# Cluster attention on one core: four of six first tiles split on GpSimd, and masks, v's splits, moves and loads placed anew

## The chip, the cores and the metric

The program runs on one core of a Trainium2 chip. The time is device microseconds of one execution; before the change the median of three runs is 765.99 us (765.26 to 767.38). The core has five engines with a queue each: TensorE (PE, with its weight loads shown apart as PEld), VectorE (DVE), ScalarE (ACT), GpSimd (POOL) and SyncE (SP), which here only issues DMAs.

## The reference

Three stages follow each other. Attention has 2 batches, 8 heads, 768 rows and a head dimension of 64; a row of q sees only rows of k that fall to the same of 16 centroids. Then come two feed-forward stages on 1536 tokens.

```python
mask = q_assign[:, :, :, None] == k_assign[:, :, None, :]
scores = scale * np.matmul(q, k.transpose(0, 1, 3, 2))
scores = np.where(mask, scores, -1000000000.0)
scores = scores - np.max(scores, axis=-1, keepdims=True)
attn = np.exp(scores)
attn = attn / (np.sum(attn, axis=-1, keepdims=True) + 1e-09)
x = np.matmul(attn, v)            # heads side by side: 1536 x 512
x = (x @ w1) * (x @ w2) @ w3 @ w_out
gate = 1.0 / (1.0 + np.exp(-(x @ w_gate)))
out = gate * (x @ w_val) @ w_out2
```

q_assign and k_assign are the arg max of the similarity of a normalised row with the normalised centroids.

## The kernel before

Every product is made of values that are split in a high part, rounded to fp32r, and a low part, the rest; a product is high x high + high x low + low x high. A split is two instructions: a cast or copy, and a subtraction.

**Pairs and blocks.** Two heads of a batch make a pair, so there are 8 pairs (pr). A pair has two heads (e = 0, 1) and each head three groups of 256 rows of q, so a pair has 6 blocks, numbered at = 0 to 5, and the program 48 (i). What is called "block 4 of pair 1" below is i = 10. The loop over i writes out by hand the order of every engine's instructions; no scheduler changes it, and each engine works its queue in this order.

**One block.** PE makes scores s of 128 rows of q against all 768 of k twice a block (scores, L313 to L316), for rows that are 1.5 blocks ahead. DVE takes the row maximum (maxima, nm, L323), ACT the exponential (exponentials, e, L334). PE turns e in three tiles of 256 columns of k by 256 rows, k2 = 0, 1, 2 (transposes, pt, L344). Each tile is split: ACT casts the high part ph (L362) and DVE subtracts for the low part pl (L373). Where by_pool says so, ACT copies the tile to pc (L359) and GpSimd makes both parts (split, L54 and L59); before, that is tile k2 = 0 of blocks 1, 2 and 4. One block later PE multiplies both parts with v (weighted_v, av, L385 and L386). Scores go to two PSUM buffers, so new scores wait for the exponential of those two before; turned tiles have three buffers, pc has one.

**What goes on beside the blocks.** During a pair the next pair's mask and the last pair's x are made, in steps that are tied to a block:

- For the next pair: DVE turns the similarities (prep_sum, sT), GpSimd adds high and low (prep_add, sm, L252), DVE finds the largest (prep_argmax, mx and sm, L259 and L260), GpSimd gives it a code (prep_code, L265), DVE makes a one-hot of it (prep_onehot, mc and oh) and turns it (prep_turn, ohT, L277), GpSimd scales a part (prep_mask, L291), and SP moves it into 32 more rows of the operands QH and KH (QH<-ohT, KH<-ohT). A pair's scores start in block 4 of the pair before it, and need these rows.
- prep_scatter moves the parts of q and k to the operands of each head, six DMAs a head. load_v loads v (vraw, one buffer for both heads); prep_v splits it on GpSimd, one head at a time (vx).
- For the last pair: join_x moves half of each head's result to other partitions (xa, xb, three DMAs), add_x and norm_x add and scale (L436 and L440), spread loads the inverse sums (r) into xb's buffer, split_x makes the parts that the next stage reads. All arithmetic of it is GpSimd's.
- convert makes weights of the next stage ready, in five steps (f64_steps: w_a, w_f, L93 to L111), one weight a pair. prep_split splits q and k of the pair after the next (hi, lo).

SP's queue is in order as well: a move that waits for its source or its target holds all behind it.

**The last stage.** quads makes products of one of six groups (M) of two factors (w) out of seven smaller ones. combined puts them together on DVE: total (L984, L989, L990) frees the PSUM bank, hi is a cast on ACT and lo a subtraction on DVE (u, L997). A list (then) says how many items later each is issued.

Of the kernel before, what the change touches and what calls it, by code (L numbers as in the profile page):

```python
# [8 lines left out]
F32 = mybir.dt.float32  # L9
# [6 lines left out]
B, H, S, D, C = 2, 8, 768, 64, 16  # L16
# [11 lines left out]
def tile_cluster_attention__then__moe__then__gated_moe(  # L28
# [20 lines left out]
    NPR = B * NP  # L49
# [11 lines left out]
    def move(dst, src):  # L61
        nc.sync.dma_start(dst.bitcast(F32), src.bitcast(F32))
# [232 lines left out]
    def prep_v(pr, e):  # L295
        vx = core.tile([128, KT, 2, D], F32R, tag="vx", name=f"vx{pr}_{e}", bufs=3)
        split(raw[pr, "v"][:, e], vx[:, :, e, :], vx[:, :, 1 - e, :], nc.gpsimd, nc.gpsimd)
        opnd[pr, e, "v"] = vx
# [47 lines left out]

    def by_pool(i, k2):

        return k2 == 0 and i % 6 in (1, 2, 4)

    def split_hi(i, k2):
        if (i, k2) not in pts:
# [42 lines left out]

    ALL, FIRST, LAST = slice(0, S), slice(0, 512), slice(512, S)

    def join_x(pr):
        acc_x[pr, "xb"] = core.tile([128, S], F32, tag="xb", name=f"xb{pr}", bufs=1)
        xa, x1, xb = acc_x[pr, 0], acc_x[pr, 1], acc_x[pr, "xb"]  # L400
        move(xb[0:64], xa[64:128])
        move(xb[64:128], x1[0:64])
        move(xa[64:128], x1[64:128])

# [136 lines left out]

    CONVERT = {}
    for n in range(4):
        for slot in ((n + 2, 0, 1), (n + 2, 1, 1), (n + 2, 3, 0), (n + 3, 2, 0)):
            CONVERT[slot] = n
    if True:
        prep_v(0, 0)
        for i in range(-2, NB + 2):
            pr, at = divmod(i, 6)
            nxt = pr + 1 if 0 <= i and pr + 1 < NPR else None  # L550
            later = nxt + 1 if nxt and nxt + 1 < NPR else None

            scores(2 * i + 3)
            split_hi(i - 1, 2)
            transposes(i, 0)
            if i == NB - 1:
                turn_sums(pr, ps_t.tile([128, 2, 256], F32, tag="t", name=f"rp{pr}")[:, 0, 0:128])
            first = nxt and at == 0
            if first:
                split_lo(i - 1, 2)  # L560
                prep_sum(nxt)
            maxima(2 * i + 3)
            if i == NB - 1:
                store_sums(pr)
            if nxt and at == 1:
                prep_code(nxt)
            if nxt and at == 1:
                prep_scatter(nxt, 1)
            if later and at == 0:
                load_qk(later)  # L570
            if at == 2 and 0 < pr and i < NB:
                join_x(pr - 1)
            split_lo(i - 1, 2)
            split_hi(i, 0)
            split_lo(i, 0)
            if nxt and at == 3:
                for e in range(2):
                    prep_mask(nxt, e)
            if (pr, at, 0) in CONVERT:
                convert(CONVERT[pr, at, 0])  # L580
            if 0 < pr and i < NB and at == 5:
                norm_x(pr - 1)
                split_x(pr - 1)
            if nxt and at == 2 + (nxt == 1):
                prep_v(nxt, 0)
            if 0 < pr and i < NB and at == 3:
                add_x(pr - 1)
                spread(pr - 1, "xb", 1)
            exponentials(2 * i + 3)
            if 0 <= i < NB and at == 4:  # L590
                guard_sums(pr)
            if later and at == 3:
                halves = prep_split(later)
                next(halves)
            if later and at == 4:
                for _ in halves:
                    pass
            weighted_v(i - 1, 0)
            weighted_v(i - 1, 1)
            if i == 0:  # L600
                prep_scatter(1, 0)
            if later and at == 5:
                prep_scatter(later, 0)
            if at == 2 and 0 < pr < 5:
                convert(pr - 1)

            scores(2 * i + 4)
            turning = 0 <= i < NB - 1 and at == 5
            if turning:
                turn_sums(pr, sps[2 * i + 4][:, S : S + 128])  # L610
            if nxt and at == 0:
                prep_add(nxt)
            if 0 < pr < NPR and at == 0 or i == 1:
                prep_v(pr, 1)
            if nxt and at == 0:
                load_v(nxt)
            transposes(i, 1)
            split_hi(i, 1)
            weighted_v(i - 1, 2)
            transposes(i, 2)  # L620
            take_x(i - 1)
            maxima(2 * i + 4)
            if turning:
                store_sums(pr)
            split_lo(i, 1)
            exponentials(2 * i + 4)
            if 0 <= i < NB and at == 4:
                invert(pr)
            if i == -1:
                prep_sims(1)  # L630
            if nxt and at == 0:
                prep_argmax(nxt)
            if nxt and at == 1:
                prep_onehot(nxt)
            if nxt and at == 2:
                prep_turn(nxt)
            if (pr, at, 1) in CONVERT:
                convert(CONVERT[pr, at, 1])
            if later and at == 5:
                prep_sims(later)  # L640
            if i == NB - 2:
                end_move(0)
            if i == NB:
                end_move(1, FIRST)
                spread(END, "raw", 3)
                end_add(0)
        end_move(1, LAST)
        end_add(1, FIRST)
        end_norm(FIRST)
        end_split(FIRST)  # L650
        end_add(1, LAST)
        end_norm(LAST)
        end_split(LAST)
# [314 lines left out]
    def quads(M, w, between=None):  # L968
# [10 lines left out]
        def combined(p, unit, mt, src, n):  # L979
            g = gate(p, unit, mt)  # L980

            def total():
                if w == 0:
                    nc.vector.tensor_tensor(out=g, in0=src, in1=s[n, p], op=ALU.add)  # L984
                    return
                c = src
                if n is not None:
                    c = s[n, p]
                    nc.vector.tensor_tensor(out=c, in0=src, in1=c, op=ALU.add)  # L989
                nc.vector.tensor_tensor(out=g, in0=c, in1=g, op=ALU.mult)  # L990

            def hi():
                nc.scalar.copy(u_of(M, p, unit, mt)[:, 0], g)

            def lo():
                u = u_of(M, p, unit, mt)
                nc.vector.tensor_tensor(out=u[:, 1], in0=g, in1=u[:, 0], op=ALU.subtract)  # L997

            if w == 0 and n is None:
                then(lambda: nc.scalar.activation(g, src, AF.Sigmoid))  # L1000
            elif w == 0:
                then(total)
                then(lambda: nc.scalar.activation(g, g, AF.Sigmoid), 2)
            else:
                then(total)
                then(hi, 3)
                then(lo, 4, 2)

        for n, step in enumerate("a0 a1 b0 b1 c0 c1 d0 e0 d1 e1 g0 f0 g1 f1".split()):
            f, p = step[0], int(step[1])  # L1010
# [179 lines left out]
```

## Time and profile before

| what | us |
|---|---|
| median of three runs | 765.99 |
| the profiled execution, whole | 764.99 |
| its span, first to last instruction | 763.2 |
| PE busy | 745.7 |
| DVE busy | 572.6 |
| ACT busy | 472.0 |
| GpSimd busy | 407.8 |

The profile tells each instruction's start, duration and engine, and what ended the idle time ahead of it. PE's times are modelled from when matmuls enter, so its busy time is an upper bound; idle time ahead of a matmul is a wait. The granted TensorE clock is 0.999 of full speed over the whole span. The rows that the prediction uses stand in a section of their own below. In a row, out<-in are tiles of the program by name, for all buffers alike, and [idle <-releaser] is how long the engine was idle ahead of this instruction, and what ended that.

### The profile page before, as it was taken

How to read it: one execution, taken by the hardware profiler on the slowest of the kernel's cores; microseconds unless marked ns; L12 is line 12 of the kernel's file. 1: busy time of each engine (PE TensorE's matmuls, PEld its weight loads, DVE VectorE, ACT ScalarE, POOL GpSimd, SP SyncE). 2: the span in 40 equal slices, each digit the busy share in tenths (PEclk: the TensorE clock that was granted, in tenths of full speed). 3: DMA queues.
4: the chain of work that ended last, by engine and by line, in shares of the span. 5: the costliest groups of instructions: out<-in, count | busy, mean ns of one | idle time of the engine just before them, and what ended most of it. 6: DMA issues, size and time to landing. Idle time of an engine off the chain costs nothing.

```text
span 763.2 us, 12228 instructions
## 1 busy us (share of the span) xinstructions
PE 745.7 (98%) x4277; PEld 679.5 (89%) x4277; DVE 572.6 (75%) x889; ACT 472.0 (62%) x994; POOL 407.8 (53%) x413
## 2 busy tenths in 40 slices
PE   7989999999999999999999999999999999999998
PEld 7888998989998888888888999998999999999996
DVE  6889999999986666567663386676687878869674
ACT  4778889889885555554542355667756555564630
POOL 3647688788764454424231036675646646375510
PEclk9999999999999999999999999999999999999999
DMA  7868677776523434333440001221302213031004
GB/s 204 205 154 213 180 204 189 206 188 163 144 60 104 145 118 137 120 130 118 134 135 1 1 1 55 83 83 56 110 2 84 83 56 111 6 127 35 29 0 166
DMA packets 29134, 82.84 MB, mean 109 GB/s; under 512 B 4848, under 2 KB 5264, under 8 KB 29072
## 3 DMA queue, kind: packets, MB, share of 16 engines
q1 hardware_dynamic: 29072, 82.05, 36.6%
q8 instruction: 34, 0.56, 0.3%
q14 instruction: 28, 0.23, 0.1%
HBM read 52.49 MB, written 3.19 MB: 73 GB/s over the span
## 4 chain that ended last, share of the span: by engine, by line
PE 79%; DVE 9%; ACT 6%; issue 3%; POOL 2%; DMA 1%; DVEq 0%; POOLq 0%; ACTq 0%
PE p L67 13%; PE p L66 13%; PE p L65 13%; PE p_a L66 4%; PE p_a L67 4%; PE p_a L65 4%; PE pt L344 3%; ACT e L334 2%; PE p_b L65 2%; DVE nm L323 2%; PE p_b L66 2%; PE p_b L67 2%; ACT ph L362 2%; DVE pl L373 2%; PE w34p L66 2%
## 5 line engine op out<-in xcount | busy, mean ns | idle before, releaser
L334 ACT ACTIVATE e<-s,nm 128x768 f32<-128x768 f32 x96 | 88.2, 919 | 15.8 <-DVE nm L323 15.3
L323 DVE TENSOR_REDUCE nm<-s 128x1 f32<-128x768 f32 x96 | 90.4, 943 | 7.6 <-PE s L316 7.4
L373 DVE TENSOR_TENSOR pl<-pt,ph 128x512 fp32r<-128x512 f32 x120 | 80.8, 684 | 13.5 <-ACT ph L362 10.1
L344 PE MATMUL pt<-ident,e 128*128 128x128 f32 x576 | 86.0, 272 | 0.0
L385 PE MATMUL av<-ph,vx 128*128 128x256 f32 x288 | 81.0, 309 | 0.4 <-POOL pl L59 0.3
L65 PE MATMUL p<-x,w 128*128 128x512 f32 (+1 forms) x208 | 80.0, 385 | 0.0
L67 PE MATMUL p<-x,w 128*128 128x512 f32 (+1 forms) x208 | 80.0, 385 | 0.0
L66 PE MATMUL p<-x,w 128*128 128x512 f32 (+1 forms) x208 | 80.0, 385 | 0.0
L362 ACT CAST ph<-pt 128x512 fp32r<-128x512 f32 x120 | 69.1, 595 | 16.6 <-PE pt L344 16.6
L386 PE MATMUL av<-pl,vx 128*128 128x256 f32 x288 | 73.9, 286 | 2.1 <-DVE pl L373 1.8
L344 PEld LDWEIGHTS pt<-ident,e 128*128 128x128 f32 x576 | 67.7, 140 | 4.1
L106 POOL TENSOR_TENSOR w_a<-w_f 128x512 uint32<-128x512 uint32 x32 | 34.7, 1085 | 64.4 <-DVE w_f L105 35.6
L1069 DVE TENSOR_TENSOR acc<-p,acc 128x512 f32<-128x512 f32 x60 | 41.2, 687 | 29.9 <-PE p L67 29.7
L976 ACT COPY s<-p_a 128x384 f32<-128x384 f32 x72 | 34.6, 481 | 42.8 <-PE p_a L67 42.5
L898 POOL TENSOR_TENSOR wgv_a<-wgv_f 128x512 uint32<-128x512 uint32 x24 | 25.3, 1055 | 66.6 <-DVE wgv_f L897 38.6
L386 PEld LDWEIGHTS av<-pl,vx 128*128 128x128 f32 x288 | 54.7, 190 | 4.3 <-DVE pl L373 4.2
L67 PE MATMUL p<-wo,u 128*128 128x512 f32 x144 | 57.0, 396 | 0.0
L66 PE MATMUL p<-wo,u 128*128 128x512 f32 x144 | 56.7, 394 | 0.0
L65 PE MATMUL p<-wo,u 128*128 128x512 f32 x144 | 56.0, 389 | 0.0
L385 PEld LDWEIGHTS av<-ph,vx 128*128 128x128 f32 x288 | 54.4, 189 | 0.8 <-POOL pl L59 0.5
L313 PE MATMUL s<-KH,QH 96*128 96x512 f32 x96 | 42.5, 442 | 7.3 <-ACT e L334 3.0
L65 PEld LDWEIGHTS p<-x,w 128*128 128x128 f32 x208 | 39.0, 188 | 7.5
(247 smaller groups left out, 2285.2 us busy)
## 6 DMA issues: line engine op xcount, KB each, us to landing
wgv_f<-in_w_gv_dram SPq DMA_DIRECT2D x24, 512.0 KB, 3.2
wo_f<-in_w_out_dram SPq DMA_DIRECT2D x20, 512.0 KB, 3.3
w_f<-in_w_dram SPq DMA_DIRECT2D x16, 512.0 KB, 3.2
w_f<-in_w3T_dram SPq DMA_DIRECT2D x16, 512.0 KB, 3.2
raw<-in_qkT_dram SPq DMA_DIRECT2D x16, 384.0 KB, 3.8
r<-r_dram SPq DMA_DIRECT2D x16, 192.0 KB, 3.6
out_dram<-acc SPq DMA_DIRECT2D x12, 256.0 KB, 2.1
xb<-xa SPq DMA_DIRECT2D x15, 192.0 KB, 3.7
```

Of the source, the lines that this page charges most:

```text
L65: nc.tensor.matmul(ps, whi, xhi, start=start, stop=False, skip_group_check=more)
L66: nc.tensor.matmul(ps, whi, xlo, start=False, stop=False, skip_group_check=more)
L67: nc.tensor.matmul(ps, wlo, xhi, start=False, stop=stop, skip_group_check=more)
L313: nc.tensor.matmul(sp[:, 0:512], QH[:, q], KH[:, 0:512], start=True, stop=False)
L323: nc.vector.tensor_reduce(out=nms[j], in_=sps[j][:, 0:S], axis=AX.X, op=ALU.max, negate=True)
L334: nc.scalar.activation(et, sps.pop(j)[:, 0:S], AF.Exp, bias=nms.pop(j), accum_out=acc_x[pr, "sum"][:, at : at + 1])
L344: nc.tensor.transpose(pt[:, kk, 128 * t : 128 * t + 128], exps[2 * i + t][:, k0 : k0 + 128], ident)
L362: nc.scalar.copy(ph, pt)
L373: nc.vector.tensor_tensor(out=pl, in0=src, in1=ph, op=ALU.subtract)
L385: nc.tensor.matmul(avs[i], w, ph[:, kk, :], start=kt == 0, stop=False)
L386: nc.tensor.matmul(avs[i], w, pl[:, kk, :], start=False, stop=kt == KT - 1)
L1069: nc.vector.tensor_tensor(out=acc[:, t, :], in0=bk, in1=acc[:, t, :], op=ALU.add)
```

## The change

Four of six first tiles, of blocks 0, 1, 3 and 4, are split on GpSimd, instead of three, of 1, 2 and 4. prep_mask comes ahead of block 3's tiles. prep_turn comes ahead of a low part of its block. v's splits move: head 1 of a pair from block 0 to block 2, head 0 of the next pair from block 2 or 3 to block 5; the load of v moves from block 0 to block 4. The moves of x go from block 2 to blocks 0 and 1, the add from block 3 to block 2. For the first pair, the moves of the next pair's head 1 go from block 1 behind head 0's mask in block 3. The load of a weight moves from block 2 to block 3, and its fourth step to the end of block 3. In the last stage the low parts of the first group move from four to seven items later.

```diff
--- before.py
+++ after.py
@@ -346,7 +346,7 @@
 
     def by_pool(i, k2):
 
-        return k2 == 0 and i % 6 in (1, 2, 4)
+        return k2 == 0 and i % 6 in (0, 1, 3, 4)
 
     def split_hi(i, k2):
         if (i, k2) not in pts:
@@ -395,10 +395,12 @@
 
     ALL, FIRST, LAST = slice(0, S), slice(0, 512), slice(512, S)
 
-    def join_x(pr):
-        acc_x[pr, "xb"] = core.tile([128, S], F32, tag="xb", name=f"xb{pr}", bufs=1)
+    def join_x(pr, e):
+        if e == 0:
+            acc_x[pr, "xb"] = core.tile([128, S], F32, tag="xb", name=f"xb{pr}", bufs=1)
         xa, x1, xb = acc_x[pr, 0], acc_x[pr, 1], acc_x[pr, "xb"]
-        move(xb[0:64], xa[64:128])
+        if e == 0:
+            return move(xb[0:64], xa[64:128])
         move(xb[64:128], x1[0:64])
         move(xa[64:128], x1[64:128])
 
@@ -541,7 +543,7 @@
 
     CONVERT = {}
     for n in range(4):
-        for slot in ((n + 2, 0, 1), (n + 2, 1, 1), (n + 2, 3, 0), (n + 3, 2, 0)):
+        for slot in ((n + 2, 0, 1), (n + 2, 1, 1), (n + 2, 3, 1), (n + 3, 2, 0)):
             CONVERT[slot] = n
     if True:
         prep_v(0, 0)
@@ -564,27 +566,32 @@
                 store_sums(pr)
             if nxt and at == 1:
                 prep_code(nxt)
-            if nxt and at == 1:
-                prep_scatter(nxt, 1)
             if later and at == 0:
                 load_qk(later)
-            if at == 2 and 0 < pr and i < NB:
-                join_x(pr - 1)
+            if at == 0 and 0 < pr and i < NB:
+                join_x(pr - 1, 0)
+            if at == 1 and 0 < pr and i < NB:
+                join_x(pr - 1, 1)
+            if nxt and nxt > 1 and at == 1:
+                prep_scatter(nxt, 1)
+            if nxt and at == 3:
+                for e in range(2):
+                    if nxt == e == 1:
+                        prep_scatter(1, 1)
+                    prep_mask(nxt, e)
             split_lo(i - 1, 2)
             split_hi(i, 0)
             split_lo(i, 0)
-            if nxt and at == 3:
-                for e in range(2):
-                    prep_mask(nxt, e)
             if (pr, at, 0) in CONVERT:
                 convert(CONVERT[pr, at, 0])
             if 0 < pr and i < NB and at == 5:
                 norm_x(pr - 1)
                 split_x(pr - 1)
-            if nxt and at == 2 + (nxt == 1):
-                prep_v(nxt, 0)
+            if 0 < pr < NPR and at == 2:
+                prep_v(pr, 1)
+            if 0 < pr and i < NB and at == 2:
+                add_x(pr - 1)
             if 0 < pr and i < NB and at == 3:
-                add_x(pr - 1)
                 spread(pr - 1, "xb", 1)
             exponentials(2 * i + 3)
             if 0 <= i < NB and at == 4:
@@ -601,7 +608,7 @@
                 prep_scatter(1, 0)
             if later and at == 5:
                 prep_scatter(later, 0)
-            if at == 2 and 0 < pr < 5:
+            if at == 3 and 0 < pr < 5:
                 convert(pr - 1)
 
             scores(2 * i + 4)
@@ -610,9 +617,11 @@
                 turn_sums(pr, sps[2 * i + 4][:, S : S + 128])
             if nxt and at == 0:
                 prep_add(nxt)
-            if 0 < pr < NPR and at == 0 or i == 1:
+            if nxt and at == 5:
+                prep_v(nxt, 0)
+            if i == 1:
                 prep_v(pr, 1)
-            if nxt and at == 0:
+            if nxt and at == 4:
                 load_v(nxt)
             transposes(i, 1)
             split_hi(i, 1)
@@ -622,6 +631,8 @@
             maxima(2 * i + 4)
             if turning:
                 store_sums(pr)
+            if nxt and at == 2:
+                prep_turn(nxt)
             split_lo(i, 1)
             exponentials(2 * i + 4)
             if 0 <= i < NB and at == 4:
@@ -632,8 +643,6 @@
                 prep_argmax(nxt)
             if nxt and at == 1:
                 prep_onehot(nxt)
-            if nxt and at == 2:
-                prep_turn(nxt)
             if (pr, at, 1) in CONVERT:
                 convert(CONVERT[pr, at, 1])
             if later and at == 5:
@@ -1004,7 +1013,7 @@
             else:
                 then(total)
                 then(hi, 3)
-                then(lo, 4, 2)
+                then(lo, 4 if M else 7, 2)
 
         for n, step in enumerate("a0 a1 b0 b1 c0 c1 d0 e0 d1 e1 g0 f0 g1 f1".split()):
             f, p = step[0], int(step[1])
```

The order of GpSimd's instructions shows two of these. First before, from the first tile of block 4 of pair 3 into block 0 of pair 4 (lo: k's low part for a later pair; xa, x: the last pair's x; sm: the sum of similarities; vx: v's split).

```order
L54 TENSOR_SCALAR ph_0_1979<-pc_1981 128x512
L59 TENSOR_TENSOR pl_0_1980<-pc_1981,ph_0_1979 128x512
L59 TENSOR_TENSOR lo_1_1990<-raw_1_1680,hi_1_1989 128x768
L440 TENSOR_TENSOR xa_0_1348<-xa_0_1348,r_1918 128x768
L54 TENSOR_SCALAR x<-xa_0_1348 128x768
L59 TENSOR_TENSOR x<-xa_0_1348,x 128x768
L252 TENSOR_TENSOR sm_2160<-sT_2132 128x384
L54 TENSOR_SCALAR vx_1_2162<-vraw_1707 128x6x64
L59 TENSOR_TENSOR vx_1_2162<-vraw_1707,vx_1_2162 128x6x64
```

Now the same stretch after the change.

```order
L54 TENSOR_SCALAR ph_0_1982<-pc_1984 128x512
L59 TENSOR_TENSOR pl_0_1983<-pc_1984,ph_0_1982 128x512
L59 TENSOR_TENSOR lo_1_1993<-raw_1_1686,hi_1_1992 128x768
L442 TENSOR_TENSOR xa_0_1353<-xa_0_1353,r_1916 128x768
L54 TENSOR_SCALAR x<-xa_0_1353 128x768
L59 TENSOR_TENSOR x<-xa_0_1353,x 128x768
L54 TENSOR_SCALAR vx_0_2088<-vraw_2010 128x6x64
L59 TENSOR_TENSOR vx_0_2088<-vraw_2010,vx_0_2088 128x6x64
L54 TENSOR_SCALAR ph_0_2150<-pc_2152 128x512
L59 TENSOR_TENSOR pl_0_2151<-pc_2152,ph_0_2150 128x512
L252 TENSOR_TENSOR sm_2172<-sT_2140 128x384
```

Between x's low part and sm there now stand v's split for head 0 and the split of block 0's first tile.

On DVE, block 2 of pair 4 into block 3, before (nm: row maximum; pl: low part of tile 1 or 2; ohT: the turned one-hot):

```order
L323 TENSOR_REDUCE nm_2286<-s_2273 128x1
L373 TENSOR_TENSOR pl_2_2279<-pt_2_2257,ph_2_2278 128x512
L323 TENSOR_REDUCE nm_2341<-s_2318 128x1
L373 TENSOR_TENSOR pl_1_2329<-pt_1_2323,ph_1_2328 128x512
L277 STREAM_TRANSPOSE ohT_2346<-oh 128x768
L323 TENSOR_REDUCE nm_2361<-s_2348 128x1
```

And after:

```order
L323 TENSOR_REDUCE nm_2295<-s_2282 128x1
L373 TENSOR_TENSOR pl_2_2288<-pt_2_2266,ph_2_2287 128x512
L373 TENSOR_TENSOR pl_0_2299<-pt_0_2290,ph_0_2298 128x512
L323 TENSOR_REDUCE nm_2342<-s_2319 128x1
L277 STREAM_TRANSPOSE ohT_2344<-oh 128x768
L373 TENSOR_TENSOR pl_1_2330<-pt_1_2324,ph_1_2329 128x512
L323 TENSOR_REDUCE nm_2362<-s_2349 128x1
```

A low part of tile 0 (pl_0) has come in, and ohT stands ahead of pl_1 and not behind it.

On DVE in the last stage, the end of the first group's second factor, before (gate: the product that frees a bank; u: a low part):

```order
L990 TENSOR_TENSOR gate_1_3989<-s_1_3_1_6340,gate_1_3989 128x384
L997 TENSOR_TENSOR u_0_0_6330<-gate_0_3986,u_0_0_6330 128x384
L990 TENSOR_TENSOR gate_1_3987<-p_0_1_a_3991,gate_1_3987 128x384
L997 TENSOR_TENSOR u_0_1_6342<-gate_1_3987,u_0_1_6342 128x384
L989 TENSOR_TENSOR s_1_2_0_6275<-p_0_1_b_3993,s_1_2_0_6275 128x384
L990 TENSOR_TENSOR gate_0_3986<-s_1_2_0_6275,gate_0_3986 128x384
L997 TENSOR_TENSOR u_1_0_6356<-gate_0_3988,u_1_0_6356 128x384
```

And after:

```order
L999 TENSOR_TENSOR gate_1_4005<-s_1_3_1_6356,gate_1_4005 128x384
L999 TENSOR_TENSOR gate_1_4003<-p_0_1_a_4007,gate_1_4003 128x384
L998 TENSOR_TENSOR s_1_2_0_6291<-p_0_1_b_4009,s_1_2_0_6291 128x384
L999 TENSOR_TENSOR gate_0_4002<-s_1_2_0_6291,gate_0_4002 128x384
L999 TENSOR_TENSOR gate_1_4005<-p_0_1_a_4008,gate_1_4005 128x384
L1006 TENSOR_TENSOR u_0_0_6346<-gate_0_4002,u_0_0_6346 128x384
```

The first low part stood ahead of the product of p_a; it now stands three rows behind it.

## Rows read from the trace of the kernel before

**Rows 1.** Busy time by stretch: start:end, length, each engine's busy us.

```profile
0.00:240.00 240.00, 227.25 (x1670) 211.17 (x1671) 212.63 (x312) 197.75 (x427) 165.76 (x160) 1.00 0.66 170
240.00:764.00 524.00, 518.49 (x2609) 468.34 (x2607) 359.92 (x577) 274.27 (x568) 242.08 (x254) 1.00 0.24 80
sum 764.00, PE 745.73 PEld 679.51 DVE 572.55 ACT 472.02 POOL 407.84; mean PE 372.87 PEld 339.75 DVE 286.28 ACT 236.01 POOL 203.92
```

**Rows 2.** Groups of PE, 38 to 160 us: xcount | busy us, mean ns | idle us.

```profile
L313 PE MATMUL s<-KH,QH 96*128 96x512 f32 x52 | 22.9, 440 | 5.3 <-DMA KH<-ohT 2.1 <-ACT e L334 1.4 <-ACT ph L362 1.1
```

**Rows 3.** PE in order of time: start us, us, instruction, [idle <-releaser].

```profile
43.00 0.47 PE L313 MATMUL s<-KH,QH 96*128 96x512 f32 x1 [2.12 <-DMA KH<-ohT]
...
67.35 0.48 PE L313 MATMUL s<-KH,QH 96*128 96x512 f32 x1
...
208.05 0.48 PE L313 MATMUL s<-KH,QH 96*128 96x512 f32 x1
```

**Rows 4.** GpSimd in order of time, block 4 of pair 3 into pair 4.

```profile
127.50 0.62 POOL L54 TENSOR_SCALAR ph<-pc 128x512 fp32r<-128x512 f32 x1
128.21 1.87 POOL L59 TENSOR_TENSOR pl<-pc,ph 128x512 fp32r<-128x512 f32 x1
...
134.69 1.84 POOL L59 TENSOR_TENSOR x<-xa,x 128x768 fp32r<-128x768 f32 x1
137.07 1.01 POOL L252 TENSOR_TENSOR sm<-sT 128x384 f32<-128x384 f32 x1 [0.54 <-DVE sT L246]
138.05 0.51 POOL L54 TENSOR_SCALAR vx<-vraw 128x384 fp32r<-128x384 f32 x1
138.64 1.01 POOL L59 TENSOR_TENSOR vx<-vraw,vx 128x384 fp32r<-128x384 f32 x1
...
143.53 1.29 POOL L59 TENSOR_TENSOR pl<-pc,ph 128x512 fp32r<-128x512 f32 x1
...
152.90 1.04 POOL L106 TENSOR_TENSOR w_a<-w_f 128x512 uint32<-128x512 uint32 x1 [0.96 <-DVE w_f L105]
```

**Rows 5.** DVE in order of time, block 1 of pair 4.

```profile
139.97 0.54 DVE L259 TENSOR_REDUCE mx<-sm 128x24 f32<-128x384 f32 x1
```

**Rows 6.** Groups of DVE, 107 to 191 us: three pairs.

```profile
L323 DVE TENSOR_REDUCE nm<-s 128x1 f32<-128x768 f32 x36 | 33.7, 937 | 0.0
L373 DVE TENSOR_TENSOR pl<-pt,ph 128x512 fp32r<-128x512 f32 x45 | 30.3, 684 | 5.2 <-ACT ph L362 4.0
...
L277 DVE STREAM_TRANSPOSE ohT<-oh 128x768 f32<-128x768 f32 x3 | 2.9, 968 | 0.0
L105 DVE SCALAR_TENSOR_TENSOR w_f<-w_f,w_a 128x512 uint32<-128x512 uint32 x3 | 2.0, 672 | 0.0
...
L273 DVE TENSOR_TENSOR oh<-sm,mc 128x384 f32<-128x384 f32 x3 | 1.7, 557 | 0.1
...
L259 DVE TENSOR_REDUCE mx<-sm 128x24 f32<-128x384 f32 x3 | 1.6, 542 | 0.0
L102 DVE TENSOR_SCALAR w_a<-w_a 128x512 uint32<-128x512 uint32 x3 | 1.3, 419 | 0.0
```

**Rows 7.** ACT in order of time, end of block 3 of pair 4.

```profile
151.00 0.90 ACT L334 ACTIVATE e<-s,nm 128x768 f32<-128x768 f32 x1 [0.42 <-DVE nm L323]
...
152.62 0.57 ACT L362 CAST ph<-pt 128x512 fp32r<-128x512 f32 x1
```

**Rows 8.** DVE and PE in order of time, last stage.

```profile
511.67 1.09 DVE L997 TENSOR_TENSOR u<-gate,u 128x384 fp32r<-128x384 f32 x1
...
513.28 0.44 PE L65 MATMUL p_a<-x,a 128*128 128x384 f32 x1 [0.76 <-DVE gate L990]
...
515.81 0.45 PE L65 MATMUL p_b<-x,a 128*128 128x384 f32 x1 [0.15 <-DVE gate L990]
```

**Rows 9.** GpSimd and DVE in order of time, block 2 of pair 0.

```profile
30.63 1.03 POOL L59 TENSOR_TENSOR vx<-vraw,vx 128x384 fp32r<-128x384 f32 x1
30.67 1.40 DVE L273 TENSOR_TENSOR oh<-sm,mc 128x384 f32<-128x384 f32 x1
```

## The prediction

> **What bounds the kernel now.** I read the busy times by stretch first [rows 1]. Their sum row gives PE 98%, DVE 75% and GpSimd 53% of 764 us. A PE at 98% by modelled ends says little, so the two stretches matter: the attention takes the first 240 us and the rest 524. In the rest PE is idle 524 - 518.5 = 5.5 us, a good part of that after the last matmul, and the only waits after the attention's end are the two of [rows 8]. In the attention PE is idle 240 - 227.3 = 12.7 us. That is the stock from which a gain can come.
>
> Most of it is the first scores of a pair. Of the idle time before L313 between 38 and 160 us, 5.3 us [rows 2], nearly all lies at five places, one a pair, in block 4. The longest is at 43.00 us, 2.12 us, and ended by the landing of KH<-ohT [rows 3]: the mask rows of the next pair came late. The rest is in blocks 1 and 2, where PE waits for a low part from DVE.
>
> Then I asked what paces a pair. From block 4 of pair 1 to block 4 of pair 6, 67.35 to 208.05 us [rows 3], five pairs take 140.7, so 28.1 each. GpSimd runs without a pause from the split of block 4 (127.50) to the end of x's low part, 134.69 + 1.84 = 136.53, so 9.03 us [rows 4], and then waits for DVE before it adds the similarities (sm, 137.07). That sum ends at 138.08, and DVE asks for it only at 139.97 (mx) [rows 5]. So GpSimd has 1.9 us of slack there, and the diff fills exactly this place.
>
> **The change part by part.**
>
> *One more first tile on GpSimd.* In each of eight pairs DVE loses one pl, 0.68 us, or 0.61 from start to start. ACT's copy stays as long as the cast was. GpSimd gets 0.62 for the high part and 1.29 for the low one [rows 4].
>
> *Where it goes.* Block 0 now gives its tile to GpSimd, in front of sm. v's e = 0 split (0.51 and 1.01) stands in front of that, since it moved from block 2 to block 5. The add on xa left the queue ahead of block 4's split, but that split waits for ACT's copy anyway, so it hardly starts sooner. From the start of block 4's split to the end of sm, GpSimd therefore needs 9.03 + 0.51 + 1.01 + 0.62 + 1.29 + 1.01 with small hand-offs: 13.5 us in one piece, where it was 10.6 with a wait in it. DVE comes to mx 0.6 us sooner than before and finds sm some 2 us late.
>
> *What is queued behind mx.* The next row maximum on DVE, hence an exp, hence PE's scores of block 2, since there are two score buffers. I follow this as a cycle, because it closes. After sm, DVE has up to the maximum of block 3: four short steps (0.54 to 0.56), five maxima (0.94), five pl (0.68), w_a (0.42) and ohT (0.97) [rows 6]. That is 2.2 + 4.7 + 3.4 + 0.4 + 1.0 = 11.7; each starts some 0.06 before the one before it ends, 15 times, so 10.8. The pl that left block 0 is back here, in block 2, and ohT now stands ahead of a pl. Then ACT's exp and the high part of the next q: 152.62 - 151.00 = 1.62 to the start of the cast, 0.57 for it [rows 7]. Then pl (0.61), w_f (0.67) and GpSimd's w_a (1.04) [rows 4, 6], 4.6 with hand-offs, and GpSimd is at block 4's split again. Sum: 13.5 + 10.8 + 4.6 + 0.1 = 29.0 us a pair, against 28.1. Into pair 6 there is no weight to convert: 28.5. Five pairs: 4 x 29.0 + 28.5 = 144.5, against 140.7: **+3.8**. In this sum PE's stalls for the mask have gone, and what is late next is sm.
>
> Bounds: if the cycle is not closed, because some link starts early, a pair falls towards what is left when the mask waits go, 28.1 less about 0.8. If GpSimd is slowed as in the rows of the port below, it is 29.8.
>
> *Masks, moves of x, loads.* Up to block 4 of pair 1 GpSimd has no x to finish, so its queue is light. There the 2.12 us at 43.00 go, because six moves of e = 1 no longer stand before the mask moves on SP, and v's load, which held SP until GpSimd had freed its buffer, moves behind them. Against it, ohT ahead of a pl (0.97) and the extra pl in block 2 (0.68) make PE wait there; of these 1.65 I take 0.6 in each of pairs 0 and 1, since DVE has about 1 us free by then. So **-2.1 + 1.2 = -0.9**. Bounds: -2.1 and +1.2. SP's queue: the moves of x leave block 2, where the third waited for the landing of the first, and come in blocks 0 and 1, where the second waits for ACT's last copy; behind it stand e = 1's moves, not needed before block 3. The convert's load and r go behind the masks and have more than a block of time. The five mask waits after 67.35 are inside the cycle already and are not counted again.
>
> *Low parts of u later.* At 513.28 and 515.81 PE waits 0.76 and 0.15 for DVE's product on the gate, in front of which stands a low part of u (1.09 us) [rows 8]. Four such parts of the first group move three items back, so the product comes about 1 us earlier: **-0.9**. They are needed only when the first output tiles start, several items later. Bounds: 0, if DVE is late from before, and -1.2 with the slower first matmuls after a wait.
>
> Sum: +3.8 - 0.9 - 0.9 = **+2.0 us**. The profiled execution took 764.99, its span 763.2; it becomes 767.0. The median of the runs shown, 765.99, lies 1.0 above it, so I forecast **768.0**.
>
> **A rule weighed against the rows.** In pair 0 DVE's one-hot compare (oh) took 1.40 us, where three later ones took 0.56 each; a GpSimd v split ran beside it from 30.63 [rows 6, 9]. Block 4's low part takes 1.87 on GpSimd and others 1.29 [rows 4]. The Trainium skill, "SBUF — State Buffer", section "Who interferes with whom", says that a VectorE instruction with two SBUF inputs contends with a GpSimd instruction that reads SBUF, and that the one that comes second is blocked, not slowed. The trace agrees in that both lengthen. By that rule the moved pl, with an input in PSUM, cost nobody anything, while its two GpSimd pieces can stand in DVE's way.
>
> **Rivals.**
>
> *GpSimd comes in time (faster).* If sm is ready when DVE asks, the cycle doesn't bind and the mask waits simply vanish: 5.3 [rows 2] and 0.9 go, 765.99 - 6.2 = 759.8. For it: GpSimd is busy only 53% [rows 1] and DVE has time free in every pair. Against it: those 13.5 us are one queue in order. It decides if the chain is 2 us shorter than I sum.
>
> *The two engines collide (slower).* GpSimd now works through nearly the whole pair, so DVE's steps with two SBUF inputs meet its splits more often. One meeting a pair on the cycle costs 1.40 - 0.56 = 0.84; over five pairs 4.2, so 772.2. For it: [rows 9]. Against it: in my order of the cycle GpSimd waits for DVE just while oh runs. It decides from the first meeting a pair that lies on the cycle.
>
> *The cycle is real but shorter.* Every link is 0.1 or so shorter and a pair takes 28.6: the two sides balance, 766.0.
>
> **How the numbers follow.** A measurement of this kernel tells a difference from no change at about 0.3%, 2.3 us: 763.7 to 768.3. Forecast 0.42, from 766.5 to 769.7, of which 0.30 is within that and 0.12 slower. GpSimd in time 0.25: 0.24 faster, 0.01 within. Collision 0.20, slower. Shorter cycle 0.13: 0.11 within, 0.02 faster. Together faster 0.26, within 0.42, slower 0.32. The range leaves out the faster half of the first rival and the far end of the second: 760.5 to 772.5. The forecast alone has 766.5 to 769.7.
>
> **What would show it.** Right: no wait for KH<-ohT or in front of L313 in block 4 worth over 0.5 us; DVE's mx waits for GpSimd's sm by 1 to 2.5 us in pairs 2 to 6; scores of block 2 wait for an exp; a pair takes 28.6 to 29.4 from block 4 to block 4; no wait of PE near 513 us. Wrong: mx starts without a wait, or a pair takes 27.5 or less. A DVE compare of over 1 us in pairs 2 to 6 would speak for the collision.

## The result and the profile after

The kernel after takes 771.24 us (median of 6, 770.31 to 771.42), the kernel before 765.62 beside it (6 runs, 764.57 to 767.41): ratio 1.0067, 95% interval 1.0051 to 1.0083. It is slower by 0.7%, more than twice what can be told from no change. The forecast was 768.0, with a range of 760.5 to 772.5. The result lies inside this range, near its slow end, and outside the 766.5 to 769.7 of the case that was held likeliest. One execution of e9 below took 920.12 us at a granted clock of 0.754 and stands in no ratio.

The profiled execution took 771.34 us, against 764.99 before, so 6.35 more. The two groups of PE on which most turns, 38 to 160 us, for [rows 2] (xcount | busy us, mean ns | idle us in front of them):

```profile
L386 PE MATMUL av<-pl,vx 128*128 128x256 f32 x152 | 40.0, 291 | 6.0 <-DVE pl L373 5.4
L313 PE MATMUL s<-KH,QH 96*128 96x512 f32 x50 | 22.0, 441 | 0.0
```

The waits for masks in front of the scores [rows 2] have all gone: 5.3 became 0.0. In their place the weighted sum of v waits 6.0 for low parts, nearly all of them DVE's (0.9 before).

GpSimd from block 4 of pair 3 to sm of pair 4, in order of time, for [rows 4]:

```profile
129.52 0.62 POOL L54 TENSOR_SCALAR ph<-pc 128x512 fp32r<-128x512 f32 x1
130.23 1.87 POOL L59 TENSOR_TENSOR pl<-pc,ph 128x512 fp32r<-128x512 f32 x1
...
136.72 1.84 POOL L59 TENSOR_TENSOR x<-xa,x 128x768 fp32r<-128x768 f32 x1
138.53 0.51 POOL L54 TENSOR_SCALAR vx<-vraw 128x384 fp32r<-128x384 f32 x1
139.12 1.02 POOL L59 TENSOR_TENSOR vx<-vraw,vx 128x384 fp32r<-128x384 f32 x1
140.11 0.62 POOL L54 TENSOR_SCALAR ph<-pc 128x512 fp32r<-128x512 f32 x1
140.81 1.29 POOL L59 TENSOR_TENSOR pl<-pc,ph 128x512 fp32r<-128x512 f32 x1
142.06 1.03 POOL L252 TENSOR_TENSOR sm<-sT 128x384 f32<-128x384 f32 x1
```

No row has a wait. The piece takes 143.09 - 129.52 = 13.57 us. DVE at its end, for [rows 5]:

```profile
141.28 0.69 DVE L373 TENSOR_TENSOR pl<-pt,ph 128x512 fp32r<-128x512 f32 x1 [0.34 <-ACT ph L362]
143.12 0.55 DVE L259 TENSOR_REDUCE mx<-sm 128x24 f32<-128x384 f32 x1 [1.15 <-POOL sm L252]
143.71 0.56 DVE L260 TENSOR_TENSOR sm<-sm,mx 128x384 f32<-128x384 f32 x1
144.18 0.95 DVE L323 TENSOR_REDUCE nm<-s 128x1 f32<-128x768 f32 x1
145.05 0.68 DVE L373 TENSOR_TENSOR pl<-pt,ph 128x512 fp32r<-128x512 f32 x1
```

mx waits for sm, and behind it stands the low part that PE wants next. PE in order of time, for [rows 3, 8]: waits in block 1 of pairs 1, 4 and 7 (58.07, 145.79, 229.12), the starts of block 4 of pairs 1 and 6 (67.57, 213.59), and the one wait in the last stage:

```profile
58.07 0.38 PE L386 MATMUL av<-pl,vx 128*128 128x256 f32 x1 [1.09 <-DVE pl L373]
...
67.57 0.48 PE L313 MATMUL s<-KH,QH 96*128 96x512 f32 x1
...
145.79 0.39 PE L386 MATMUL av<-pl,vx 128*128 128x256 f32 x1 [1.13 <-DVE pl L373]
...
213.59 0.48 PE L313 MATMUL s<-KH,QH 96*128 96x512 f32 x1
...
229.12 0.39 PE L386 MATMUL av<-pl,vx 128*128 128x256 f32 x1 [0.89 <-POOL pl L59]
...
527.49 0.51 PE L67 MATMUL p<-wo,u 128*128 128x512 f32 x1 [0.26 <-DVE u L1006]
```

Four terms make the difference. Up to block 4 of pair 1: 67.57 - 67.35 = +0.2. Five pairs: 213.59 - 67.57 = 146.0 against 140.7, +5.3. The rest of the attention +1.7: block 4 of pair 6 is 0.55 longer and block 1 of pair 7 is 1.16 longer. The last stage, from block 4 of pair 7 (240.36, before 233.12) to the end: -0.9. Sum 6.3.

Two more waits bear on these terms. At 50.81 GpSimd stands for v, whose load comes behind the six moves of e = 1 on SP; at 220.84 it stands for r:

```profile
50.81 0.51 POOL L54 TENSOR_SCALAR vx<-vraw 128x384 fp32r<-128x384 f32 x1 [4.56 <-DMA vraw<-in_v_dram]
...
88.84 1.32 POOL L59 TENSOR_TENSOR vx<-vraw,vx 128x384 fp32r<-128x384 f32 x1
...
220.84 1.84 POOL L442 TENSOR_TENSOR xa<-xa,r 128x768 f32<-128x768 f32 x1 [2.83 <-DMA r<-r_dram]
```

And in pair 2 a step of DVE (0.42 in the other three places) runs beside the v split of 88.84:

```profile
88.72 0.56 DVE L273 TENSOR_TENSOR oh<-sm,mc 128x384 f32<-128x384 f32 x1
89.19 1.26 DVE L102 TENSOR_SCALAR w_a<-w_a 128x512 uint32<-128x512 uint32 x1
```

### The profile page after: what moved, and what is told of

Same layout as the page of the kernel before. It is cut to its first block, busy times and chain, and to the rows that moved or that the text cites. A ratio compares the mean times of both kernels' runs of the same rounds, so it can differ in the third digit from the quotient of the medians.

```text
span 769.6 us, 12240 instructions
## 1 busy us (share of the span) xinstructions
PE 749.5 (97%) x4277; PEld 680.2 (88%) x4277; DVE 566.6 (74%) x881; ACT 472.2 (61%) x994; POOL 423.3 (55%) x429
## 4 chain that ended last, share of the span: by engine, by line
PE 70%; DVE 10%; POOL 9%; issue 4%; ACT 4%; DMA 2%; SPq 1%; POOLq 0%; ACTq 0%; DVEq 0%
PE p L67 13%; PE p L66 13%; PE p L65 13%; PE p_a L66 4%; PE p_a L67 4%; PE p_a L65 4%; DVE nm L323 3%; PE p_b L66 2%; PE p_b L67 2%; PE p_b L65 2%; DVE pl L373 2%; PE w34p L67 2%; PE w34p L66 2%; PE w34p L65 2%; POOL pl L59 2%
## 5 line engine op out<-in xcount | busy, mean ns | idle before, releaser
L373 DVE TENSOR_TENSOR pl<-pt,ph 128x512 fp32r<-128x512 f32 x112 | 75.1, 682 | 16.9 <-ACT ph L362 15.8
L386 PE MATMUL av<-pl,vx 128*128 128x256 f32 x288 | 75.5, 291 | 10.9 <-DVE pl L373 8.7
L386 PEld LDWEIGHTS av<-pl,vx 128*128 128x128 f32 x288 | 54.6, 190 | 15.6 <-DVE pl L373 13.5
L362 ACT CAST ph<-pt 128x512 fp32r<-128x512 f32 x112 | 64.1, 591 | 5.5 <-PE pt L344 5.5
L1078 DVE TENSOR_TENSOR acc<-p,acc 128x512 f32<-128x512 f32 x60 | 41.2, 687 | 29.8 <-PE p L67 29.3
L59 POOL TENSOR_TENSOR pl<-pc,ph 128x512 fp32r<-128x512 f32 x32 | 44.7, 1396 | 2.7
```

Source lines behind the costliest of these rows:

```text
L59: lo_engine.tensor_tensor(out=lo, in0=x, in1=hi, op=ALU.subtract)
L362: nc.scalar.copy(ph, pt)
L373: nc.vector.tensor_tensor(out=pl, in0=src, in1=ph, op=ALU.subtract)
L386: nc.tensor.matmul(avs[i], w, pl[:, kk, :], start=False, stop=kt == KT - 1)
L1078: nc.vector.tensor_tensor(out=acc[:, t, :], in0=bk, in1=acc[:, t, :], op=ALU.add)
```

## The experiments

Ratios are to the kernel before, with 95% intervals; by "block n" is meant the stretch of PE from its scores to those of the next block. Where nothing is late a block takes 4.16 us. The kernel before was run again beside each set of experiments: its median lay between 765.62 and 767.24, single executions between 764.55 and 769.76 (the last section shows what most of this scatter goes with). Differences between changed kernels are therefore taken from their times, not by way of that median.

**Is it the place ahead of sm, or the load?** An add of 128x384 was put on GpSimd, the same in both kernels: once just ahead of sm (shown), once in block 2, ahead of v's split.

```
+            if nxt and pr and at == 0:
+                nc.gpsimd.tensor_tensor(out=extra, in0=extra, in1=extra, op=ALU.add)
             if nxt and at == 0:
                 prep_add(nxt)
```

> The changed kernel with one more GpSimd instruction in each of pairs 1 to 6, an addition on a tile of its own (128x384, about 1.0 us by the rows of that size), just ahead of sm in block 0. Theory A: it lies on the path, so each of six pairs becomes 1.0 longer: 776.8 (775 to 778). Rival L: as much as the same instruction in block 2 costs (next kernel).

> The changed kernel with the same extra GpSimd instruction (128x384, 1.0 us) in pairs 1 to 6, but in block 2, where GpSimd then waits about 2 us for ACT's or DVE's next step. Theory A: it is off the path, 0 to 0.5 us: 771.5 (770.5 to 772.5). Rival L: the same work for the same engine, so as much as the kernel with it ahead of sm, 773 to 777 for both.

Measured: ahead 778.88 us (1.0152, 1.0137 to 1.0167), aside 771.45 (1.0057, 1.0041 to 1.0073). DVE with the add ahead (lines are two further on):

```profile
147.12 0.55 DVE L261 TENSOR_REDUCE mx<-sm 128x24 f32<-128x384 f32 x1 [1.92 <-POOL sm L254]
```

The two places differ by 7.4 us for the same work, and aside it costs next to nothing (0.2 more than the kernel after). So the queue up to sm is a bound, and GpSimd's load by itself is not.

But the 7.4 are not six times one price. Against the kernel after, pairs 2, 3 and 5 are each 0.77 longer in block 1, pair 1 is 1.56 longer, and pairs 4 and 6 are 2.2 and 2.0 longer. PE's wait in block 1 of pairs 3 and 4, then three stretches around the one in pair 4 and one of pair 6 (of a stretch: length, PE busy, granted clock, DMA share, GB/s):

```profile
119.86 0.39 PE L388 MATMUL av<-pl,vx 128*128 128x256 f32 x1 [1.93 <-DVE pl L375]
149.79 0.38 PE L388 MATMUL av<-pl,vx 128*128 128x256 f32 x1 [1.93 <-DVE pl L375]
146.00:150.00 4.00, 2.07 (x16) 1.00 0.49 100
150.20:153.50 3.30, 3.30 (x15) 0.50 0.97 210
153.60:157.00 3.40, 3.40 (x27) 1.00 0.83 179
211.70:215.00 3.30, 3.30 (x16) 0.50 0.77 168
```

PE waits 1.93 in both pairs (1.16 and 1.13 in the kernel after). In pairs 4 and 6 the granted clock then falls to 0.50, the lower of its two levels (1.2 and 2.4 GHz), and these pairs pay 1.2 to 1.4 us more than the other three. In the kernel after the clock doesn't fall in the attention.

**sm ahead of the extra tile**, in the kernel after (the call goes from its place behind the scores to the front of the splits).

```
+            if nxt and at == 0:
+                prep_add(nxt)
             split_lo(i - 1, 2)
             split_hi(i, 0)
             split_lo(i, 0)
```

> The changed kernel with one thing moved: in block 0 GpSimd adds the similarities (sm) ahead of the split of the first tile, not behind it. The work of every engine is the same. Theory A (sm's place in GpSimd's queue sets the pace: DVE's mx waits 1.1 us for it in pairs 1 to 6): sm comes 1.95 us earlier, mx no longer waits, the first tile's low part comes 1.0 later and PE waits up to 0.8 for it in block 1; a pair takes 28.0 to 28.3 and not 29.2, the whole 765.5 (764 to 767). Rival L (GpSimd simply has too much work, or its port meets DVE more often, whatever the order): 771, within 1.

Measured: 768.85 us, 1.0024 (1.0015 to 1.0033): 2.4 us come back, not all. mx no longer waits. DVE, then GpSimd, then PE of this kernel:

```profile
140.49 0.54 DVE L259 TENSOR_REDUCE mx<-sm 128x24 f32<-128x384 f32 x1
141.07 1.02 DVE L260 TENSOR_TENSOR sm<-sm,mx 128x384 f32<-128x384 f32 x1
```

```profile
138.71 1.02 POOL L252 TENSOR_TENSOR sm<-sT 128x384 f32<-128x384 f32 x1
139.69 0.62 POOL L54 TENSOR_SCALAR ph<-pc 128x512 fp32r<-128x512 f32 x1
140.39 1.28 POOL L59 TENSOR_TENSOR pl<-pc,ph 128x512 fp32r<-128x512 f32 x1
```

```profile
141.72 0.39 PE L386 MATMUL av<-pl,vx 128*128 128x256 f32 x1 [0.58 <-POOL pl L59]
```

The tile that was moved back is now itself late (PE waits 0.58 for it), and its low part runs beside DVE's sm, which takes 1.02 and not 0.56.

**The fourth tile taken away**, in the kernel after.

```
-        return k2 == 0 and i % 6 in (0, 1, 3, 4)
+        return k2 == 0 and i % 6 in (1, 2, 4)
```

> The changed kernel with the old choice of tiles on GpSimd, blocks 1, 2 and 4; masks, v's splits, moves of x, loads and the low parts of u stay as in the change. Theory A: nothing but v's split stands ahead of sm, so sm is there when DVE asks (4.3 us after the pair's start against 4.8), and the mask waits of the kernel before are gone too: a pair takes about 27.5, the whole 762.5 (761 to 765). Rival L expects a gain too, since 1.9 us of GpSimd's work a pair go. A rival P, that the new places of v's splits, moves and masks are what costs: it stays above 768.

Measured: 766.08 us, 0.9999 (0.9984 to 1.0013); the 761 to 765 of theory A did not come. The wait for DVE's pl goes (L386: 1.8 us from 40 to 225 us, 8.8 in the kernel after, 1.3 in the kernel before), but the mask waits are back. Up to 225 us (the profiled execution, 768.94, is the slowest of twelve):

```profile
L313 PE MATMUL s<-KH,QH 96*128 96x512 f32 x77 | 34.2, 444 | 6.9 <-DMA KH<-ohT 5.2 <-ACT ss L414 1.8
```

So, by the medians, the choice of four tiles costs 5.2 us against the old three, and the rest of the change alone brings nothing: in the trace GpSimd's ohT stands behind v's split and its add on xa (119.52 to 121.37, ohT at 121.46).

**The meeting of DVE and GpSimd in pair 2.** One step of the first conversion goes from block 1 to block 2.

```
-            CONVERT[slot] = n
+            CONVERT[(2, 2, 0) if slot == (2, 1, 1) else slot] = n
```

> The changed kernel with one DVE step moved: in pair 2 the second step of the weight's conversion (w_a, 1.26 us there and 0.42 in later pairs) goes from the end of block 1 to block 2, behind the first tile, where GpSimd is past v's split. If it was long because both engines were at SBUF at the same time, it takes about 0.4 there and block 2 of pair 2 takes 4.5 instead of 5.33: the whole 0.8 less, 770.4. Rival: the first conversion is long for another reason (its data lands late): it stays at 1.2 or block 2 stays at 5.3.

Measured: 771.07 us, 1.0056 (1.0036 to 1.0076). The step met GpSimd again, with its add on xa (90.31 to 92.18):

```profile
91.45 1.03 DVE L102 TENSOR_SCALAR w_a<-w_a 128x512 uint32<-128x512 uint32 x1
```

Block 2 of pair 2 went from 5.33 to 4.15, block 3 from 4.53 to 5.49. The edit moved the meeting and didn't remove it, so by the time the two theories stay undivided. In the trace the step is long in each place where it meets GpSimd, and the block is long with it.

**Low parts of u, alone**, in the kernel before.

```
-                then(lo, 4, 2)
+                then(lo, 4 if M else 7, 2)
```

> The kernel before with one part of the change: the low parts of u of the first group seven items later instead of four. My step: the waits of 0.76 and 0.15 at 513 and 516 us go: 0.9 less, 0.6 to 1.4, so about 764.7 where before is 765.6. Rival: DVE only shifts them into the next products, and a wait of the same size appears there: no difference.

Measured: 766.34 us against 767.24, 0.9991 (0.9975 to 1.0008): 0.9 is what was forecast, but the interval holds zero. The two waits of [rows 8] are gone from the trace, and one of 0.25 comes at 522.57, in front of the first output tile. From block 4 of pair 7 to the end the trace takes 529.15 us, where the kernel before takes 530.10; in the traces of after, e2 and e7, which have the same edit, it is 529.15 to 529.19.

**sm first, v's split and load nearly as before**, in the kernel after (core of the edit).

```
+            if nxt and at == 2:
+                load_v(nxt)
+            if nxt and at == 0:
+                prep_add(nxt)
...
-            if 0 < pr < NPR and at == 2:
-                prep_v(pr, 1)
+            if nxt and at == 3:
+                prep_v(nxt, 0)
...
+            if 0 < pr < NPR and at == 0 or i == 1:
+                prep_v(pr, 1)
```

> The changed kernel, four tiles on GpSimd, with sm ahead of block 0's split, v's head 1 behind that split in block 0 and v's head 0 of the next pair in block 3 behind the mask and the tile, its load in block 2. GpSimd has as much work as in the change, but only the add and the tile stand between x and v. Theory A: neither mx nor the first low part waits: 758 (756.5 to 761). Rival L (too much work on GpSimd): above 766.

Measured: 768.84 us, 1.0028 (1.0017 to 1.0039), no better than with sm alone ahead. mx doesn't wait, block 1 is 4.57, but block 2 is 5.10, where PE waits for the next tile that GpSimd splits:

```profile
148.00 0.39 PE L386 MATMUL av<-pl,vx 128*128 128x256 f32 x1 [0.56 <-POOL pl L59]
```

Here theory A fails: in each of the three orders of the four tiles so far (after, e1, e8) PE waits in pairs 2 to 5 for something that came late through GpSimd.

**v's load of pair 1 two blocks earlier.**

```
-            if nxt and at == 4:
+            if nxt and at == 4 - 2 * (nxt == 1):
                 load_v(nxt)
```

> Base: the kernel after, with v's load of pair 1 issued in block 2 and not in block 4 of pair 0, so ahead of the masks and of the six moves of e = 1 on SP. Theory V (the part of the first stretch that the forecast missed comes from that load: GpSimd stands 4.56 us before v's split at 50.81, and all behind it, sm of pair 1 too, is late): GpSimd doesn't stand there, mx of pair 1 doesn't wait, block 1 of pair 1 goes from 5.50 to 4.4, and 1.1 us is gone: 770.1 us. Rival X (block 1 of pair 1 is long from the extra pl on DVE and GpSimd's own queue, whatever the load does): block 1 of pair 1 stays at 5.3 to 5.6, 771.2 us.

Measured: 769.89 us, 1.0044 (1.0028 to 1.0060). GpSimd's v split and sm of pair 1:

```profile
46.23 0.51 POOL L54 TENSOR_SCALAR vx<-vraw 128x384 fp32r<-128x384 f32 x1
...
53.29 1.03 POOL L252 TENSOR_TENSOR sm<-sT 128x384 f32<-128x384 f32 x1
```

Block 1 of pair 1 goes from 5.50 to 4.43; mx doesn't wait there. That is the miss of the first stretch. The span shrinks by 1.6; the other 0.5 is block 1 of pair 7 (5.32 to 4.79), which wasn't expected.

**Masks ahead, without the fourth tile.** The kernel before, with the moves of x in blocks 0 and 1, the first pair's moves for head 1 behind head 0's mask, the weight's load in block 3 and its fourth step at that block's end, the low parts of u later, and, in every pair, v's split for head 0 in block 3 behind GpSimd's mask step and not in block 2 ahead of it (core of the edit):

```
             if nxt and at == 3:
                 for e in range(2):
+                    if nxt == e == 1:
+                        prep_scatter(1, 1)
                     prep_mask(nxt, e)
+            if nxt and at == 3:
+                prep_v(nxt, 0)
+            if 0 < pr and i < NB and at == 3:
+                add_x(pr - 1)
...
-            if nxt and at == 2 + (nxt == 1):
-                prep_v(nxt, 0)
```

> The kernel before, with its three tiles on GpSimd and its place of v's head 1, plus the parts of the change that bear on the masks: x's moves in blocks 0 and 1, the first pair's head 1 moves behind head 0's mask, masks ahead of v's split and of the add of x, the weight's load in block 3 and its fourth step at that block's end, and u's low parts later. sm then has the place it had. Theory A: the 5.3 us that PE waited for masks go and nothing new comes on the path: 765.6 - 5.3 - 0.9 = 759.4 (758 to 762). Rival: the waits for masks only hid others, DVE's low parts in blocks 1 and 2 above all: 763 to 766.

Measured: 763.39 us, 0.9956 (0.9940 to 0.9971): faster than both kernels, but in the range of the rival, 763 to 766, and not in that of theory A. PE from 38 to 160 us:

```profile
L386 PE MATMUL av<-pl,vx 128*128 128x256 f32 x158 | 40.9, 288 | 2.9 <-DVE pl L373 2.8
L313 PE MATMUL s<-KH,QH 96*128 96x512 f32 x52 | 22.9, 440 | 0.0
```

The mask waits are gone here too, and the waits for DVE's pl have grown from 0.9 to 2.9, as the rival has it. A pair with a conversion takes 28.7, pair 1, without one, 27.0; block 4 is 4.97 with it and 4.16 without.

**The conversion's step half a block earlier.** In that kernel (e7), the fourth step stands where the kernel before has it; e12 is the same kernel as e9.

```
-        for slot in ((n + 2, 0, 1), (n + 2, 1, 1), (n + 2, 3, 1), (n + 3, 2, 0)):
+        for slot in ((n + 2, 0, 1), (n + 2, 1, 1), (n + 2, 3, 0), (n + 3, 2, 0)):
```

> Base: e7_masks_alone, with one step of the conversion of a weight half a block earlier (middle of block 3 again, where the kernel before has it, and not its end). In e7 a pair takes 28.7 us with a conversion, 27.0 without; its block 4 takes 4.97 there, with a wait of 0.55 of PE for DVE's pl, its block 2 4.71. Theory S (that wait is DVE being late by the conversion's step, which stands just ahead): block 4 goes to 4.16 to 4.3 in pairs 2 to 5, a pair to 28.0, 3 us less in all: 760.3 us (759.3 to 761.3). Rival K (DVE and GpSimd have a fixed amount to do there, and the wait moves to another block): block 3 or 4 is still 0.8 longer, 763.4 us.

> The kernel of e9_masks_step once more, for a profile at the full granted clock (its time is known: 763.5 us). e9 took as long as e7, so block 4's 0.8 us must be somewhere else. Theory K (what DVE and GpSimd have to do moves with the step): block 4 is down to 4.2 to 4.4, and block 3 or block 5 up by as much, with an L386 waiting for DVE's or GpSimd's pl. Rival N (the step had no part in it): block 4 still 4.97.

Measured: 763.51 us (0.9954, 0.9938 to 0.9971), and 763.49 in the one run of e12. Nothing gained: in e12's trace block 4 falls from 4.97 to 4.80, and block 5 grows from 6.14 to 6.31. The traces show a step of DVE that is long in both, in e7 first and then in e12, with GpSimd of e12 behind them:

```profile
152.11 1.36 DVE L105 SCALAR_TENSOR_TENSOR w_f<-w_f,w_a 128x512 uint32<-128x512 uint32 x1
```

```profile
150.33 1.27 DVE L105 SCALAR_TENSOR_TENSOR w_f<-w_f,w_a 128x512 uint32<-128x512 uint32 x1
```

```profile
150.04 1.02 POOL L59 TENSOR_TENSOR vx<-vraw,vx 128x384 fp32r<-128x384 f32 x1
151.02 2.28 POOL L438 TENSOR_TENSOR xa<-xa,xb 128x768 f32<-128x768 f32 x1
```

w_f takes 0.67 in the kernel before [rows 6]. In e7 it runs beside the add on xa (151.05 to 152.92), in e12 beside the v split, and is 0.6 to 0.7 longer in both; in e12 the add behind it is long as well (2.28, where e7 has 1.87). The step has a part in block 4's wait, but what it costs goes along with it.

**A fourth tile in another block**, in e9's kernel.

```
-        return k2 == 0 and i % 6 in (1, 2, 4)
+        return k2 == 0 and i % 6 in (1, 2, 4, 5)
```

> Base: e9_masks_step (763.5 us), with a fourth first tile on GpSimd, as in the kernel after, but block 5's and not block 0's. In e7_masks_alone, which differs from the base by one place of the conversion, sm is ready 1.9 us before DVE asks for it (136.39, mx 138.28), and the tile costs GpSimd 0.62 + 1.28 = 1.9 us ahead of xa, x and sm. Theory C (a tile on GpSimd costs nothing as long as it leaves sm and the masks in time, and then gives DVE back 0.61 us a pair): mx waits 0 to 0.2 us, PE's waits for DVE's pl shrink by some 0.3 to 0.6 us in each of pairs 2 to 5: 762 us (760.8 to 763.2). Rival L (GpSimd has no room for a fourth tile, wherever it stands): mx or an L386 waits 0.5 us or more for GpSimd in each pair: 766 to 768 us.

Measured: 764.67 us, 0.9974 (0.9959 to 0.9988). Neither number came. mx waits nowhere, which speaks for C, but the time is 1.2 above e9's. DVE and GpSimd behind block 5's tile:

```profile
167.91 0.55 DVE L259 TENSOR_REDUCE mx<-sm 128x24 f32<-128x384 f32 x1
168.50 1.38 DVE L260 TENSOR_TENSOR sm<-sm,mx 128x384 f32<-128x384 f32 x1
```

```profile
166.84 1.03 POOL L252 TENSOR_TENSOR sm<-sT 128x384 f32<-128x384 f32 x1
167.83 0.53 POOL L54 TENSOR_SCALAR vx<-vraw 128x384 fp32r<-128x384 f32 x1
168.44 1.03 POOL L59 TENSOR_TENSOR vx<-vraw,vx 128x384 fp32r<-128x384 f32 x1
```

sm now comes just in time (it ends at 167.87, mx starts at 167.91), so GpSimd's next steps fall beside DVE's next steps. DVE's sm takes 1.38 in place of 0.56, more than the 0.61 that the tile took off DVE, and PE waits 0.5 to 0.7 for DVE's pl in block 1 of pairs 2 to 6.

## Why the prediction was off, step by step

The direction and the mechanism were right: the mask waits went, and sm, behind 13.5 us of GpSimd's queue, came late. The size was not: +2.0 us was forecast, and the medians differ by 5.6 and the two traces, in neither of which the clock fell during the attention, by 6.3. Three terms were each too small, by 1.5, 1.1 and 1.7. That the range held them was no merit of these terms: its slow end was there for the collision, which the trace shows in one pair only.

*GpSimd's piece.* 13.5 us was summed, 13.57 came. mx waits for sm 1.10 to 1.15 in pairs 2 to 6, at the low end of the 1 to 2.5 forecast and not the "some 2 us late" of the working, and e4 against e5 shows that this queue sets the pace. The end of the mask waits was right too. (The 1.08 in pair 1 has another cause, v's load: it goes in e10.)

*What is late next.* The prediction named an exp, hence the scores of block 2. It is the low part behind mx, hence L386 in block 1 (1.06 to 1.16 a pair). The wait that it named for the extra pl and for ohT ahead of a low part is there: block 3 is 0.4 longer (4.53). It takes both, since e2, with ohT in the same place but block 2's tile on GpSimd, has 4.14 to 4.16.

*The cycle, the term that was mis-sized.* It was put at 29.0 us a pair and 28.5 into pair 6, +3.8; the trace has 29.8, 29.1, 29.2, 29.2, 28.8: +5.3. Of the 1.5 missing, 0.8 is the pair in which the second conversion step lasts 1.26 in place of 0.42, beside GpSimd's v split; that reading is of the traces, since e6 moved the meeting and saved no time. The collision rival had this price (0.84), but it was met once, not once a pair. e1 and e11 suggest why: where mx no longer waits for sm, DVE's sm runs beside GpSimd's next step and is 0.5 to 0.9 longer. The last 0.7 is spread over four pairs and was not taken apart.

*The first stretch.* -0.9 was forecast, +0.2 came. The 2.12 us did go. The step that failed is that v's load "moves behind them", counted as a gain for SP alone: v was needed at once, GpSimd stood 4.56 us for it, and sm of pair 1 came late. e10 gives back 1.1, the whole miss.

*After pair 6.* Nothing was counted there; +1.7 came. In block 4 of pair 6 (+0.55) PE waits for block 3's tile, which GpSimd splits behind v's split, the add and the mask step. In block 1 of pair 7 (+1.16) the tile stands behind a wait for r. No run was made to move that load, but it landed at other times in other runs, and the block followed it one for one: GpSimd's wait for r was 2.30, 2.36, 2.53, 2.83 and 2.88 us in e10, e5, e4, after and e1, and block 1 of pair 7 took 4.79, 4.87, 5.01, 5.32 and 5.37. That speaks for r, though it doesn't replace such a run.

*Low parts of u.* -0.9 forecast, -0.9 in the traces, e3's among them. By its time alone e3 can't be told from zero. A new wait of 0.26 stands where the low parts are needed, at 527.49.

*The rivals.* GpSimd in time (759.8) supposed that the fourth tile needs no place. No order of the four tiles tried gives it: sm first 768.85, v as before too 768.84, block 5's tile 764.67. What the change had to give comes without the tile, from the masks, now ahead of v's split, the moves and low parts of u, 0.44% (e7); in the change's own order the four tiles cost 5.2 us (e2 against after), in e11's order 1.2.

What stays open: which order, if any, lets GpSimd take four tiles and meet DVE nowhere; and which of e7's parts did how much.

## What to carry to other kernels

Before work moves to an engine with much idle time, sum its queue in order up to the next step that another engine asks for: here a micro-second ahead of that step cost 0.8 in a turn (and more where the longer wait of PE was followed by a fall of its clock), and the same work elsewhere in the turn next to nothing. A wait that goes may have kept two engines apart: after each one that is removed, look for steps that have become longer, not only for new waits. When a load is put behind other moves on a queue, ask for each instruction that it feeds, not only for those that the moves feed.

## What the runs showed of the hardware

Steps of DVE lengthen beside GpSimd's SBUF steps by nearly what is left of the other: sm of 0.56 began at 168.50, GpSimd's v split ended at 169.47, sm at 169.88 (e11), 0.41 behind it; with GpSimd's low part it was 0.42 (141.67 and 142.09, e1). It goes the other way too: the v split of 88.84 lasts 1.32, not 1.02, behind the compare that began 0.12 earlier and runs at its own 0.56. The Trainium skill, "SBUF — State Buffer", section "Who interferes with whom", says that the engine that comes first has the shared port for its whole instruction and that the other is blocked. The traces agree, but for 0.15 us: a blocked 0.56 ends 0.41 after the other. The prediction weighed only steps with two inputs in SBUF; w_a of DVE, with one, is stretched as well (0.42 to 1.26 and 1.03).

Long waits of PE can cost more than their length. In the kernel before, the times of the 24 executions beside e7 go with the granted clock: the seven at 0.999 or 1.000 took 764.74 to 766.24 us, the four at 0.995 or 0.996 768.19 to 769.33. The profile of e3, which has the masks of the kernel before, shows one such fall: behind a wait of 1.74 us for KH<-ohT at 42.62 the granted clock is 0.50 from 43.30 to 46.50. e2's shows two, behind waits in front of the scores of 1.79 and 2.15 us, and e4's two above came behind 1.93 and 1.89. A wait as long was not always followed by one (2.12 at 43.00 in the kernel before, 1.93 in pair 3 of e4). Without the mask waits all executions of after are at 1.000, and those of e7 lie between 763.33 and 763.45. So part of what e7 gains on the median of the kernel before is clock: against those seven executions it is 1.4 to 2.9 us faster, and not 3.9.
